# A banded convolution on sixteen 32-by-32 tiles of TensorE instead of four 64-by-64 ones, with the low-rank product moved behind it

## The chip, the cores and the metric

The kernel runs on one core of one Trainium2 chip. The metric is the device time of one execution in microseconds (us), as the median of several. The four runs of the kernel before lie within 0.33% of each other (352.78 to 353.95). Some executions fall in a slower state, in which the granted clock of TensorE (PE) is lower on average. A profiled execution shows a span that is about 1.8 us shorter than the time (352.1 against 353.87 for the kernel before).

## The reference

Two steps on x of 8 batches, 4224 positions and 192 channels:

```python
# 1. causal convolution: 8 heads of 24 channels, 7 softmax weights for each head
out = np.einsum('hk,bskhg->bshg', softmax(weight), x_unf)      # x_unf: 7 shifted copies of x
# 2. low-rank mixing over positions, then two dense layers over channels
h  = xt @ U @ V              # (192 x 4224) @ (4224 x 32) @ (32 x 4224), for each batch
u  = y + h.transpose(0, 2, 1)                                  # y: the convolution's result
ch = np.maximum(u @ w_ch1, 0.0) @ w_ch2                        # 192 -> 768 -> 192
return u + ch
```

## The kernel before

All matrix work is on PE in bf16. 264 tiles of 128 positions are handled in 33 groups of 8 tiles. The main loop has 34 slots. Slot `g` does the first dense layer of group `g` (`w1`), some heads of a later batch's convolution (`conv`), the second dense layer of group `g-1` (`w2`) and the low-rank product of a later group (`h_group`). The kernel holds eight PSUM banks in one pool, and every matmul group takes its bank from it in turn. ACT and DVE empty the banks.

The convolution is a product with a banded matrix: a block of positions times the band, plus a second matmul for the positions that reach over from the block before (`halo`). Before, a block has 64 positions, so a matmul uses a 64-by-64 tile of the array. The four matmuls of one `halo` lie on the four tiles (`tile_position`) and run at the same time: in the trace of before four start within 10 ns (114.091 to 114.101 us), each lasts about 0.35 us, and the next four start from 114.278 us on.

```python
    def conv(b, h, i0, i1, engs):                       # one head
        ...
        pp = [bank(), bank()]
        for halo in range(2):
            for r in range(2):
                for c in range(2):
                    st = 1 - halo + i0 + c
                    nc.tensor.matmul(
                        out=pp[r][HB * c : HB * c + HB, 0 : nn[r] * GS],
                        lhsT=band[HB * r : HB * r + HB, h, HB * halo : HB * halo + HB],
                        rhs=xt[b][HB * r : HB * r + HB, st : st + 2 * nn[r] - 1 : 2, hc],
                        start=(halo == 0), stop=(halo == 1),
                        tile_position=(HB * r, HB * c),
                    )
        ...                                             # ACT or DVE copies pp[r] into y_sb
```

Before the loop stands the prologue: loads, masks, the convolution of batch 0 in two halves, and the transposed u of groups 0 and 1. The rest of the order:

```python
    RELU = ["AA", "AD", "AA", "AD", "AD", "AD"]         # who empties w1's banks: ACT or DVE
    ...
    for k, (i0, i1) in enumerate(XCH):                  # prologue: batch 0 in two halves
        for h in range(H):
            conv(0, h, i0, i1, "AD")
        if k == 0:
            u_layout()                                  # waits for the mask Eq of POOL
            yT[0] = yT_part(0)
        tt_mm(0, ...)
    ...
    for g in range(NG + 1):
        if g + 1 < NG and g > 0:
            h_group(g + 1)                              # low-rank product, one slot ahead
            transp(g + 1)                               # transpose of u by DMA
        if g < NG:
            last = w1(g)
        ...
        for b, ch in loadq.get(g, []):                  # loads of x for a later batch
            ...
        for b, h in convq.get(g, []):
            conv(b, h, 0, NB1, "AA")
        ...
        for k in range(4):
            if g > 0:
                w2(g - 1, k)
            ...
```

## Time and profile before

| before | us |
|---|---|
| median of 3 runs (352.78 to 353.95) | 353.29 |
| profiled span | 352.1 |
| first layer of slot 0 starts | 30.00 |
| slots 0 to 4 | 50.57 |
| slots 5 to 24 | 193.48 |
| slots 25 to 31 (no convolution left but in the first) | 62.21 |
| the rest | 15.85 |

A slot is taken from the start of its first layer to the start of the next slot's. The last five lines add up to the span. All are read from the starts of PE's matmuls in the trace.

These are lines of the profile page of before: the span, PE's busy time and instruction count, the busy share and the granted clock in 40 slices of 8.8 us (tenths, 9 is 90% or more), the queue that brings instructions, and the chain of waits by engine.

```profile
span 352.1 us, 9621 instructions
...
PE 338.9 (96%) x4004; PEld 228.7 (65%) x4004; DVE 246.1 (70%) x500; ACT 191.0 (54%) x409; POOL 56.5 (16%) x98
...
PE   8589899999999999999999999999999999999995
...
PEclk9869899999999999999999999999999999999999
...
q8 instruction: 31, 0.51, 0.6%
...
PE 90%; DVE 4%; DMA 3%; POOL 2%; issue 1%; ACT 0%; POOLq 0%
```

PE is the bound: it is busy in every slice from the sixth on, and 90% of the chain lies on it. Only the first 44 us have something else to give. PE has 4004 matmuls and as many weight loads. The granted clock is below full only in the second, third and fifth slice.

Next is the timeline of PE in one steady slot of before, with two heads of convolution; the columns are start, length, engine, line, operation, and how many instructions were merged.

```profile
114.09 0.88 PE L284 MATMUL ps<-x_sb,band 64*64 64x384 bf16 x16
114.91 4.13 PE L478 MATMUL ps<-W_sb,rl_sb 128*128 128x192 bf16 x48
118.97 0.34 PE L356 MATMUL ps<-tt_sb,V_sb 32*128 32x192 bf16 x8
119.25 4.11 PE L455 MATMUL ps<-uT,W_sb 64*128 64x512 bf16 x36
123.29 0.88 PE L284 MATMUL ps<-x_sb,band 64*64 64x384 bf16 x16
```

From start to start, the convolution of two heads takes 0.82 us (114.09 to 114.91), the second layer 4.06, the product 0.28 and the first layer 4.04: 9.20 in all. There is no wait between them.

Two lines of PE's timeline in the prologue of before:

```profile
17.95 0.42 PE L256 MATMUL ps<-Ur,Eq 32*128 32x288 bf16 x1 [3.75 <-POOL Eq L151]
...
30.00 0.76 PE L455 MATMUL ps<-uT,W_sb 64*128 64x512 bf16 x4
```

PE stood for 3.75 us waiting for a mask that POOL builds, and the first layer started at 30.0 us.

### The profile page before, as it was taken

How to read it: one execution, taken by the hardware profiler on the slowest of the kernel's cores; microseconds unless marked ns; L12 is line 12 of the kernel's file. 1: busy time of each engine (PE TensorE's matmuls, PEld its weight loads, DVE VectorE, ACT ScalarE, POOL GpSimd, SP SyncE). 2: the span in 40 equal slices, each digit the busy share in tenths (PEclk: the TensorE clock that was granted, in tenths of full speed). 3: DMA queues.
4: the chain of work that ended last, by engine and by line, in shares of the span. 5: the costliest groups of instructions: out<-in, count | busy, mean ns of one | idle time of the engine just before them, and what ended most of it. 6: DMA issues, size and time to landing. Idle time of an engine off the chain costs nothing.

```text
span 352.1 us, 9621 instructions
## 1 busy us (share of the span) xinstructions
PE 338.9 (96%) x4004; PEld 228.7 (65%) x4004; DVE 246.1 (70%) x500; ACT 191.0 (54%) x409; POOL 56.5 (16%) x98
## 2 busy tenths in 40 slices
PE   8589899999999999999999999999999999999995
PEld 3354377666667776666577777666767776666675
DVE  6548865677777776666777777676677777777763
ACT  1345465776645554566666554555566644444440
POOL 8592213111101111111111110111000000000000
PEclk9869899999999999999999999999999999999999
DMA  9979989976989899878969897899445454555535
GB/s 110 193 97 158 111 165 147 205 148 152 177 169 165 176 177 181 157 135 153 185 151 180 178 184 150 169 182 177 103 114 131 121 150 118 136 137 134 136 104 166
DMA packets 122922, 53.51 MB, mean 152 GB/s; under 512 B 88160, under 2 KB 122848, under 8 KB 122880
## 3 DMA queue, kind: packets, MB, share of 16 engines
q1 hardware_dynamic: 84656, 38.18, 43.4%
q0 software_dynamic: 38224, 14.73, 37.1%
q8 instruction: 31, 0.51, 0.6%
q14 instruction: 11, 0.09, 0.1%
HBM read 29.49 MB, written 25.95 MB: 157 GB/s over the span
## 4 chain that ended last, share of the span: by engine, by line
PE 90%; DVE 4%; DMA 3%; POOL 2%; issue 1%; ACT 0%; POOLq 0%
PE ps L455 39%; PE ps L478 38%; PE ps L284 6%; DMA x_sb<-in_x_dram 3%; PE ps L356 2%; PE ps L308 2%; DVE u_sb L378 1%; DVE y_sb L299 1%; PE ps L409 1%; POOL Eq L151 1%; DVE rl_sb L467 1%; DVE uT L439 1%; POOL x_sb L76 0%; PE ps L325 0%; DVE out_sb L486 0%
## 5 line engine op out<-in xcount | busy, mean ns | idle before, releaser
L465 ACT ACTIVATE rl_sb<-ps 128x512 bf16<-128x512 f32 x264 | 133.3, 623 | 121.5 <-issue 66.2
L455 PE MATMUL ps<-uT,W_sb 64*128 64x512 bf16 x1188 | 143.6, 380 | 0.8 <-DVE uT L439 0.2
L478 PE MATMUL ps<-W_sb,rl_sb 128*128 128x192 bf16 x1584 | 138.6, 247 | 0.0
L478 PEld LDWEIGHTS <-rl_sb 128*128 128x128 bf16 x1584 | 128.8, 98 | 12.2 <-issue 12.2
L486 DVE TENSOR_TENSOR out_sb<-ps,u_sb 128x384 f32<-128x384 f32 x132 | 73.6, 557 | 77.5 <-PE ps L478 77.5
L455 PEld LDWEIGHTS <-W_sb 64*128 64x128 bf16 x1188 | 64.3, 95 | 69.2 <-issue 14.0
L467 DVE TENSOR_SCALAR rl_sb<-ps 128x512 bf16<-128x512 f32 x132 | 88.1, 689 | 7.1 <-PE ps L455 6.9
L378 DVE TENSOR_TENSOR u_sb<-y_sb,ps 128x192 bf16<-128x192 bf16 (+1 forms) x168 | 66.1, 460 | 0.0
L297 ACT ACTIVATE y_sb<-ps 128x384 bf16<-128x384 f32 (+2 forms) x128 | 52.6, 528 | 0.3
L76 POOL DMA_DIRECT2D x_sb<-in_x_dram x30 | 21.2, 705 | 178.7 <-PE ps L455 163.2
L284 PE MATMUL ps<-x_sb,band 64*64 64x408 bf16 (+3 forms) x576 | 29.5, 335 | 0.0
L284 PEld LDWEIGHTS <-band 64*64 64x64 bf16 x576 | 16.8, 117 | 13.7 <-issue 11.5
L81 POOL DMA_DIRECT2D x_sb<-in_x_dram x30 | 22.1, 736 | 0.0
L356 PE MATMUL ps<-tt_sb,V_sb 32*128 32x192 bf16 x264 | 12.8, 246 | 1.1 <-DVE u_sb L378 0.7
L356 PEld LDWEIGHTS <-V_sb 32*128 32x128 bf16 x264 | 4.8, 92 | 7.2 <-issue 6.8
L318 ACT ACTIVATE tt_hi<-ps 128x192 bf16<-128x192 f32 x9 | 3.0, 330 | 12.0 <-PE ps L308 12.0
L308 PE MATMUL ps<-y_sb,U_sb 128*32 128x192 bf16 x264 | 8.1, 254 | 0.4 <-ACT y_sb L297 0.4
L319 DVE TENSOR_TENSOR tt_lo<-ps,tt_hi 128x192 bf16<-128x192 f32 x9 | 3.2, 357 | 6.1 <-ACT tt_hi L318 6.1
L180 PE MATMUL ps<-zz 128*128 128x512 bf16 x20 | 6.0, 471 | 1.2 <-DVE zz L176 1.2
L308 PEld LDWEIGHTS <-U_sb 128*32 128x32 bf16 x264 | 5.8, 98 | 2.1 <-issue 2.0
L256 PE MATMUL ps<-Ur,Eq 32*128 32x256 bf16 (+1 forms) x16 | 2.2, 410 | 4.6 <-POOL Eq L151 4.6
L299 DVE CAST y_sb<-ps 128x192 bf16<-128x192 f32 (+1 forms) x16 | 5.1, 366 | 1.0 <-PE ps L284 1.0
(48 smaller groups left out, 55.4 us busy)
## 6 DMA issues: line engine op xcount, KB each, us to landing
out_dram<-out_sb SPq DMA_DIRECT2D x132, 192.0 KB, 2.7
x_sb<-in_x_dram POOLq DMA_DIRECT2D x42, 192.0 KB, 4.3
x_sb<-in_x_dram POOLq DMA_DIRECT2D x7, 240.0 KB, 5.5
x_sb<-in_x_dram POOLq DMA_DIRECT2D x7, 216.0 KB, 4.7
W_sb<-in_moe_w_ch_dram POOLq DMA_DIRECT2D x3, 288.0 KB, 6.0
x_sb<-in_x_dram POOLq DMA_DIRECT2D x2, 384.0 KB, 6.3
uT<-u_sb SPq DMA_TRANSPOSE x31, 3.7
x_sb<-in_x_dram POOLq DMA_DIRECT2D x1, 432.0 KB, 9.0
```

What stands on the lines that cost most here:

```text
L76: return nc.gpsimd.dma_start(out=xt[b][0:HB, 1 + i0 : 1 + e0, :], in_=x[b, i0 * HB : e0 * HB, :].rearrange("(j p) d -> p j d", p=HB),)
L81: return nc.gpsimd.dma_start(out=xt[b][HB:P, s0 : i1 + 1, :], in_=x[b, (NB0 - 1 + s0) * HB : (NB0 + i1) * HB, :].rearrange("(j p) d -> p j ...
L284: nc.tensor.matmul(out=pp[r][HB * c : HB * c + HB, 0 : nn[r] * GS], lhsT=band[HB * r : HB * r + HB, h, HB * halo : HB * halo + HB], rhs=xt ...
L297: nc.scalar.activation(out=o, in_=i, func=ACT.Copy)
L308: nc.tensor.matmul(out=p[32 * c : 32 * c + 32, 0:D], lhsT=U_sb[:, j // 4, j % 4, :], rhs=yt[b][:, j, :], start=(n < 4), stop=(n + 4 >= len ...
L356: nc.tensor.matmul(out=banks[pr][:, a * D : (a + 1) * D], lhsT=V_sb[32 * q : 32 * q + 32, (j // 8) * 2 + j % 2, :], rhs=ttb[b][32 * q : 32 ...
L378: nc.vector.tensor_tensor(out=u_group(g)[:, i : i + n, :, hf, :], in0=yt[b][:, run[0] : run[0] + n, :].rearrange("p n (c k) -> p n c k", c=3),
L455: last = nc.tensor.matmul(out=pp[hf][:], lhsT=W1_sb[HB * hf : HB * hf + HB, c, m * P : (m + 1) * P], rhs=uTt[g][HB * hf : HB * hf + HB, :, ...
L465: nc.scalar.activation(out=rl[:, m, hf, :], in_=pp[hf][:], func=ACT.Relu)
L467: nc.vector.tensor_scalar_max(out=rl[:, m, hf, :], in0=pp[hf][:], scalar1=0.0)
L478: nc.tensor.matmul(out=cps[:, a * D : (a + 1) * D], lhsT=rlt[g][:, m, hf, (i + a) * P : (i + a + 1) * P], rhs=W2_sb[:, m, :], start=(m == ...
L486: nc.vector.tensor_tensor(out=o[:].rearrange("p n (c k) -> p n c k", c=3), in0=cps[:, 0 : 2 * D].rearrange("p (n c k) -> p n c k", n=2, c= ...
```

## The change

The intent: make the convolution cheaper on PE by using all sixteen 32-by-32 tiles at once, start the first batch sooner by convolving it quarter by quarter as its loads land, and take waits out of the prologue. In the loop the product moves from ahead of the first layer to between convolution and second layer, two slots ahead. The transposed u of groups 0 and 1 is now summed in PSUM rather than by DVE. The masks are built by DVE. There are two x buffers instead of three. From batch 3 on, a batch's convolution stands one slot sooner than before and its loads two. The core of the diff, with cuts marked:

```diff
-    xs = ctx.enter_context(tc.tile_pool(name="xs", bufs=3))
+    xs = ctx.enter_context(tc.tile_pool(name="xs", bufs=2))
 ...
-    def conv(b, h, i0, i1, engs):
+    def conv(b, hp, rs, engs):                          # a pair of heads, some of the 4 quarters
 ...
-        pp = [bank(), bank()]
-        for halo in range(2):
-            for r in range(2):
-                for c in range(2):
+        pp = {r: bank() for r in rs}
+        for hh in range(2):
+            h = 2 * hp + hh
+            for halo in range(2):
+                for c in range(4):
+                    for r in rs:
+                        st = 1 - halo + c
                         nc.tensor.matmul(
+                            out=pp[r][QB * c : QB * c + QB, ...],
+                            lhsT=band[QB * r : QB * r + QB, h, QB * halo : QB * halo + QB],
+                            rhs=xt[b][QB * r : QB * r + QB, st : st + 4 * nk[r] - 3 : 4, ...],
 ...
+                            tile_position=(QB * r, QB * c),
 ...
-    RELU = ["AA", "AD", "AA", "AD", "AD", "AD"]
+    RELU = ["AD", "AD", "AA", "AD", "AD", "AD"]
 ...
+    for hp in range(4):                                 # prologue: batch 0 in quarters
+        conv(0, hp, [0], "AD"[hp % 2])
+    u_layout()
+    for hp in range(4):
+        conv(0, hp, [1], "AD"[hp % 2])
+    for hp in range(4):
+        conv(0, hp, [2], "AD"[hp % 2])
+    tt_whole(0, tt_mm(0, range(3 * NQ)), "A")
+    for hp in range(4):
+        conv(0, hp, [3], "AD"[hp % 2])
 ...
     for g in range(NG + 1):
-        if g + 1 < NG and g > 0:
-            h_group(g + 1)
-            transp(g + 1)
         if g < NG:
-            last = w1(g)
+            last = w1(g, RELU0 if g < 2 else RELU)
 ...
-            conv(b, h, 0, NB1, "AA")
+            conv(b, hp, [0, 1, 2, 3], "A")
 ...
+        for n in hq.get(g, []):                         # product, two slots ahead
+            h_group(n)
+            transp(n)
 ...
             w2(...)
```

A pair of heads now takes 64 matmuls of 192 or 216 columns where it took 16 of 384 or 408.

## The prediction

> **What bounds it now.** From about 44 us to 348 us TensorE never stops: the busy row shows PE at 95 to 100% in every slice, and the chain of waits is 90% PE (ps L455 39%, L478 38%, conv L284 6%). In the timeline a slot with two conv heads is first layer 4.03 us, conv 0.82, second layer 4.07, low-rank product 0.28: 9.2; a slot without conv takes 8.74, where the first layer waits 0.35 for banks that DVE still empties. Before 44 us the chain is made of loads, POOL's Eq masks (U layout waits for them until 20.0 us), DVE adds (uT, u_sb); the first layer starts at 30.0, its second group at 37.7.
>
> **What the change does.**
> 1. Conv: 64 matmuls of 192 or 216 columns on 16 tiles for two heads, instead of 16 of about 400 columns on 4. In the trace, matmuls on different tiles start 3.4 ns apart, and a round of 192 columns lasts 82 ns: 55 ns of issue against 82 to 93 of streaming. Two heads: 4 rounds plus a mode change, about 0.5 us instead of 0.82. 28 pairs: 9 us of PE time less (estimate). Evictions stay: 16 a batch, ACT, 0.6 us each, one per 0.38 us.
> 2. That gain should mostly turn into waits for PSUM. The product moves between conv and second layer. After the first layer PE now wants 4 banks (conv), 4 or 5 (product), then 1 (second layer), of 8. Reckoned from the slot's start with trace durations: the last relus end at 4.8 us, the conv is done at 4.63 and its first two evictions end at 5.23 and 5.6. The second layer's first bank is (by the built program) one of those: it starts at 5.28 (4-bank product) or 5.66 (5-bank), against 4.85 plus 0.28 for the product elsewhere. Slots 5 to 24: 9.3 to 9.7 us, not better than 9.2. [...] before shows no such PE wait, after should.
> 3. Slots 1 to 4 hold two pairs: eight ACT evictions in a row before the second layer, about 11.3 us instead of 9.9 in slots 3 and 4.
> 4. Slots without conv lose that wait: 8.35 us, 7 times, -2.7 us.
> 5. Prologue: masks on DVE (about 1.5 us) end the wait for Eq; band is 152 wide instead of 280 (14 ops, 0.24 instead of 0.37 us); u of the first groups accumulates in PSUM, no 0.68 us adds; the products of groups 0 and 1 no longer precede the second group. Loads land as before (x near 15 us). First layer starts near 23.5 us.
>
> **Sum.** At the fifth slot about 6 us ahead, slots 5 to 31 about 2 us lost, end 0.3 us gained: **348.0 us**, range 342.5 to 353.5. Faster by over 2%: 0.33; within 2%: 0.65; slower: 0.02.
>
> **What would show it.** Conv group under 0.6 us from its first start to the next group; PE waits at the product and the second layer, released by ACT y_sb and relus; slot time 9.3 to 9.7; first layer near 23.5 us; slots without conv near 8.35.
>
> **What would make it wrong.** Banks released earlier than reckoned (then 340 us); 16 tiles streaming slower than one round per 90 ns; x of batch 1 landing after 33 us, or batch 2's last quarter stuck on POOL's queue behind batch 3's (slower).

The "mode change" of point 1 can be read in before: 0.31 us from the last matmul of the first layer to the first of the convolution (113.784 to 114.091 us) and 0.27 us from the last of the convolution to the second layer (114.642 to 114.908), where the rounds within the convolution start 0.16 to 0.19 us apart and the pairs of first-layer matmuls ahead of it 0.215 us. The 1.5 us for the masks and the 0.24 us for an operation of the band were estimates; after has 1.6 us on DVE (five operations from 9.51 us on) and 0.24 us (ten in 2.36 us from 7.23 us on).

## The result

| | before | after |
|---|---|---|
| median of 4 runs | 353.59 | 367.38 |
| fast runs | 352.78 to 353.95 | 363.88 and 364.80 (slow: 369.97, 370.93) |
| ratio of fast runs | | 1.0307, 95% interval 1.0267 to 1.0347 |
| PE matmuls (and as many weight loads) | 4004 | 5476 |

The change made the kernel 3.1% slower. The two slow runs are left out of the ratio. A ratio is the mean time of one kernel's fast runs over that of the other's of the same rounds, so it is not quite the ratio of the medians. The profiled execution of after was one of the fast ones (363.88 us).

The same stages, from the traces:

| us | predicted | before | after | after minus before |
|---|---|---|---|---|
| first layer of slot 0 starts | near 23.5 | 30.00 | 29.78 | -0.2 |
| slots 0 to 4 | about 51 | 50.57 | 58.05 | +7.5 |
| slots 5 to 24 | | 193.48 | 197.77 | +4.3 |
| slots 25 to 31 | | 62.21 | 60.13 | -2.1 |
| slots 5 to 31 together | 2 lost | 255.69 | 257.90 | +2.2 |
| the rest | 0.3 gained | 15.85 | 16.38 | +0.5 |

The "about 51" is worked out: before is at its slot 5 at 80.57, "about 6 us ahead" is 74.5, less 23.5. So the steady part came out as predicted, in sum. (The parts as the prediction gives them, 6 and 0.3 us gained and 2 lost, make 349.0 us from 353.3, not 348.0; that is small beside the miss.) What was missed is the 88 us before it: after reaches slot 5 at 87.83 us, not 6 us ahead of before but 7.3 behind it.

The page of after, the same lines as above:

```profile
span 362.1 us, 12473 instructions
...
PE 343.7 (95%) x5476; PEld 236.8 (65%) x5476; DVE 260.4 (72%) x521; ACT 182.7 (50%) x371; POOL 35.6 (10%) x60
...
PE   8899899699999999999999999999999999999995
...
PEclk9659999889999999999999999999999999999999
...
q8 instruction: 43, 0.70, 0.8%
```

Three things differ. PE is busier in the first slices, but its clock there is lower (6 and 5 in the second and third). Slice 8 has a hole in the PE row, and the clock is below full there too. And the instruction queue brought 43 packets instead of 31, each of 16384 bytes in both traces; they are called blocks below. The chain of waits of after covers only a quarter of the span, so it is not used here.

Now PE's share of two stretches, by windows, first before, then after. The columns are the stretch, its length, PE's busy time (instructions), the granted clock, the DMA share and GB/s.

```profile
10.00:20.00 10.00, 5.12 (x71) 0.73 1.40 193
20.00:30.00 10.00, 9.05 (x176) 0.76 0.87 99
```

```profile
10.00:20.00 10.00, 9.02 (x244) 0.55 1.34 183
20.00:30.00 10.00, 9.55 (x142) 0.60 1.53 177
```

After removed the wait for the mask: PE is busy for 18.57 of these 20 us instead of 14.17. But its clock is about half. In the trace the clock is 0.5 in one piece from 10.97 to 28.04 us, 17.07 us, which is five times 3.41 us; in before the pieces at 0.5 in the first 45 us last 3.41, 6.83 and 3.41 us (from 11.12, 17.95 and 38.43 us). What that costs stands in the starts of the matmuls: four matmuls of 192 columns on the four tiles of one quarter make a round, and a round takes 82 ns at full clock (from 9.80 us) and 160 ns at half (from 12.49 us). The lines of PE's timeline of after in this stretch:

```profile
9.80 1.69 PE L282 MATMUL ps<-x_sb,band 32*32 32x192 bf16 x64
...
12.49 4.01 PE L282 MATMUL ps<-x_sb,band 32*32 32x192 bf16 x109
17.48 0.98 PE L282 MATMUL ps<-x_sb,band 32*32 32x192 bf16 x19 [0.98 <-issue]
...
19.56 3.06 PE L282 MATMUL ps<-x_sb,band 32*32 32x216 bf16 x64
22.55 1.49 PE L419 MATMUL ps<-ident,y_sb 128*64 128x128 bf16 x24
...
29.78 1.42 PE L454 MATMUL ps<-uT,W_sb 64*128 64x512 bf16 x9
```

The convolution of the last quarter alone takes 3.0 us. The 24 transposes take 1.42 us to the next group, and 0.79 us in a stretch of before where the clock is full (26.80 to 27.59). The first layer starts at 29.78.

"issue" in brackets is a wait for which the profile has no releaser. The largest such wait of after is in slot 3, here with its neighbours:

```profile
63.41 0.26 PE L282 MATMUL ps<-x_sb,band 32*32 32x192 bf16 x3
64.02 1.54 PE L282 MATMUL ps<-x_sb,band 32*32 32x216 bf16 x125 [0.35 <-DMA x_sb<-in_x_dram]
...
67.41 0.90 PE L477 MATMUL ps<-W_sb,rl_sb 128*128 128x192 bf16 x9
70.68 5.86 PE L477 MATMUL ps<-W_sb,rl_sb 128*128 128x192 bf16 x39 [2.38 <-issue]
76.48 4.06 PE L454 MATMUL ps<-uT,W_sb 64*128 64x512 bf16 x36
```

The second layer of this slot takes 9.07 us (67.41 to 76.48) instead of 4.06. 2.62 us is the stall, from one matmul start (68.06) to the next. The rest, about 2.4 us, is the clock, which the trace has at 0.5 from 69.00 to 75.83. There are three more such stalls of over 0.6 us: 1.34 at 16.13, 1.08 at 40.07 and 0.75 at 54.11.

And a steady slot of after, to be set against that of before:

```profile
108.37 4.06 PE L454 MATMUL ps<-uT,W_sb 64*128 64x512 bf16 x36
112.36 0.80 PE L282 MATMUL ps<-x_sb,band 32*32 32x192 bf16 x64
113.09 0.47 PE L367 MATMUL ps<-tt_sb,V_sb 32*128 32x192 bf16 x8
113.71 4.12 PE L477 MATMUL ps<-W_sb,rl_sb 128*128 128x192 bf16 x48
117.77 1.04 PE L454 MATMUL ps<-uT,W_sb 64*128 64x512 bf16 x8
```

The slot takes 9.40 us. The convolution takes 0.73, not the 0.5 predicted. From the start of the product to the second layer it is 0.62 us, of which the product itself took 0.28 in before: 0.34 us is a wait. The second layer starts 5.34 us after the slot; 5.28 was predicted.

### The profile page after: what moved, and what is told of

It is laid out like the page before. It is cut to its first block, busy times and chain, and to the rows that moved or that the text cites. A ratio compares the mean times of both kernels' runs of the same rounds, so it can differ in the third digit from the quotient of the medians.

```text
span 362.1 us, 12473 instructions
## 1 busy us (share of the span) xinstructions
PE 343.7 (95%) x5476; PEld 236.8 (65%) x5476; DVE 260.4 (72%) x521; ACT 182.7 (50%) x371; POOL 35.6 (10%) x60
## 5 line engine op out<-in xcount | busy, mean ns | idle before, releaser
L464 ACT ACTIVATE rl_sb<-ps 128x512 bf16<-128x512 f32 x233 | 124.5, 604 | 128.6 <-issue 73.9
L477 PEld LDWEIGHTS <-rl_sb 128*128 128x128 bf16 x1584 | 132.5, 99 | 11.5 <-issue 6.1
L454 PE MATMUL ps<-uT,W_sb 64*128 64x512 bf16 x1188 | 134.9, 377 | 0.1
L466 DVE TENSOR_SCALAR rl_sb<-ps 128x512 bf16<-128x512 f32 x163 | 107.6, 690 | 26.1 <-PE ps L454 26.1
L454 PEld LDWEIGHTS <-W_sb 64*128 64x128 bf16 x1188 | 56.2, 94 | 67.8 <-issue 6.0
L485 DVE TENSOR_TENSOR out_sb<-ps,u_sb 128x384 f32<-128x384 f32 (+1 forms) x133 | 71.0, 551 | 35.9 <-PE ps L477 35.1
L245 ACT ACTIVATE y_sb<-ps 128x384 bf16<-128x384 f32 (+1 forms) x120 | 50.7, 511 | 8.1 <-PE ps L282 6.0
L80 POOL DMA_DIRECT2D x_sb<-in_x_dram x32 | 26.0, 815 | 128.8 <-PE ps L454 113.9
L282 PEld LDWEIGHTS <-band 32*32 32x32 bf16 x2048 | 24.4, 92 | 16.2 <-issue 13.4
L282 PE MATMUL ps<-x_sb,band 32*32 32x192 bf16 (+1 forms) x2048 | 32.6, 261 | 2.2 <-issue 1.8
L367 PE MATMUL ps<-tt_sb,V_sb 32*128 32x192 bf16 x264 | 19.4, 246 | 4.4 <-ACT y_sb L245 3.4
L74 POOL MEMSET x_sb<- 32x96 uint32 x7 | 1.2, 172 | 61.7 <-PE ps L367 27.2
```

The source lines that it names most:

```text
L80: return nc.gpsimd.dma_start(out=xt[b][QB * q : QB * q + QB, s0:s1, :], in_=x[b, blk * QB : (blk + s1 - s0) * QB, :].rearrange("(j p) d -> ...
L245: nc.scalar.activation(out=out, in_=in_, func=ACT.Copy)
L282: nc.tensor.matmul(out=pp[r][QB * c : QB * c + QB, 0 : nk[r] * 2 * GS].rearrange("p (k a) -> p k a", a=2 * GS)[:, :, hh * GS : hh * GS + G ...
L367: nc.tensor.matmul(out=banks[pr][:, a * D : (a + 1) * D], lhsT=V_sb[32 * q : 32 * q + 32, (j // 8) * 2 + j % 2, :], rhs=ttb[b][32 * q : 32 ...
L454: last = nc.tensor.matmul(out=pp[hf][:], lhsT=W1_sb[HB * hf : HB * hf + HB, c, m * P : (m + 1) * P], rhs=uTt[g][HB * hf : HB * hf + HB, :, ...
L464: nc.scalar.activation(out=rl[:, m, hf, :], in_=pp[hf][:], func=ACT.Relu)
```

## The experiments

Three theories were to be told apart. A: the granted clock goes by how much of the array works, so the quarter-by-quarter convolution, which uses 4 of 16 tiles at a time, lets the clock fall although PE is busy. B: PE runs out of instructions, because the new convolution takes so many, and waits for their blocks. C: x comes late, because two buffers instead of three bunch the loads. Medians of before on the chips used were 353.28 to 354.06 us. A median below is over all runs of a kernel, and where a median holds slow runs, that is said. The stages of all runs, from their traces:

| us | first layer starts | slots 0-4 | slots 5-24 | slots 25-31 | rest | span |
|---|---|---|---|---|---|---|
| before | 30.00 | 50.57 | 193.48 | 62.21 | 15.85 | 352.1 |
| after | 29.78 | 58.05 | 197.77 | 60.13 | 16.38 | 362.1 |
| e1_hot_full | 30.06 | 55.75 | 197.76 | 60.13 | 15.99 | 359.7 |
| e2_hot_small | 34.81 | 55.78 | 197.74 | 60.12 | 15.95 | 364.4 |
| e3_xs3 | 28.80 | 54.57 | 197.75 | 60.12 | 16.57 | 357.8 |
| e4_late | 30.22 | 59.07 | 193.96 | 61.92 | 16.63 | 361.8 |
| e5_halves (slow) | 28.87 | 64.69 | 197.77 | 60.13 | 17.05 | 368.5 |
| e6_conv64 | 23.93 | 53.29 | 194.29 | 60.13 | 15.97 | 347.6 |
| e7_conv32_only | 32.50 | 52.48 | 191.71 | 62.14 | 15.86 | 354.7 |
| e8_split | 29.63 | 62.42 | 209.52 | 60.13 | 17.00 | 378.7 |
| e9_conv64_xs3 | 24.18 | 51.72 | 194.29 | 60.13 | 15.99 | 346.3 |
| e10_conv64_xs3_early | 23.63 | 50.85 | 193.13 | 61.08 | 16.01 | 344.7 |
| e11_loads_moved | 28.38 | 64.19 | 197.76 | 60.13 | 16.54 | 367.0 |
| e12_shift | 30.30 | 57.49 | 197.73 | 60.12 | 16.27 | 361.9 |

All gave correct results.

### e1_hot_full and e2_hot_small: dummy matmuls in the prologue's convolution

The changed kernel, with one matmul of zeros per bank ahead of each convolution group of batch 0. The real group overwrites what it wrote. e1 uses the whole array, e2 one 32-by-32 tile of the row group that the real matmuls use.

```diff
+        if b == 0:
+            for r in rs:
+                nc.tensor.matmul(out=pp[r][:], lhsT=zz[:, 0:P], rhs=zz[:], start=True, stop=True)
# e2: out=pp[r][0:QB, :], lhsT=zz[QB*r : QB*r+QB, 0:QB], rhs=zz[QB*r : QB*r+QB, :],
#     tile_position=(QB*r, 0)
```

> The changed kernel with one matmul of zeros on the whole array (128x128, 512 columns) before each of the 16 conv groups of the first batch, into the bank that the group then overwrites. Theory A (the clock was halved from 11 to 28 us because a conv of one quarter uses only 4 of the 16 tiles, all in one row group[...]): granted clock over 14 to 28 us at least 0.85 instead of 0.5, the conv of the second and third quarter takes under 4.5 us instead of 5.9 in spite of the extra matmuls, the first layer starts at 26 us or sooner instead of 29.8, time 2 to 5 us below the changed kernel's 364. Rival B (the engine waits for loads and evictions there, the low clock is only a sign of idling and costs nothing): first layer starts at the same 29.8 us or up to 3.5 us later, time 364 to 368.

> As e1_hot_full, but the 16 extra matmuls of zeros are 32x32 on the same row group as the conv that follows, 512 columns each: TensorE is as busy in time, the array as empty. Theory A (occupied array counts): the clock stays at 0.5 from 11 us on, the extra work runs at half speed (0.43 us each, up to 6.9 us in all), the first layer starts 2 to 7 us later than 29.8, time 366 to 371. Theory A2 (busy time counts, idling between evictions brought the clock down): the clock recovers as in e1_hot_full and the time falls like that one's.

The half speed that e2 expects (0.43 us for 512 columns) agrees with the 160 ns for 192 columns of after, which make 0.427.

Measured: e1 365.1 us (ratio 1.0289, interval 1.0221 to 1.0356), e2 367.69 (1.0406, 1.0368 to 1.0444). PE by windows, first e1, then e2:

```profile
10.00:20.00 10.00, 10.00 (x210) 1.00 1.38 192
20.00:30.00 10.00, 9.33 (x194) 1.00 1.57 183
```

```profile
10.00:20.00 10.00, 10.00 (x197) 0.58 1.37 189
20.00:30.00 10.00, 10.00 (x157) 0.50 1.61 186
```

With as many dummies, and PE busy all the time from 10 to 20 us in both (from 20 to 30 us e1 is even the less busy, 9.33 against 10.00), the clock stays full with full-array dummies and is half with small ones. In e2 the first layer starts 4.8 us later than in e1 (34.81 against 30.06). So it is not PE's busy time that holds the clock up, and the half clock costs time. Theory A stands, with one caution: a full-array dummy differs from a small one in rows and columns both, and the two were not separated. The gain that e1 was expected to show did not come, neither in the start of the first layer (30.06 us, where at most 26 was expected) nor clearly in the time: its fast runs are 361.53, 363.66 and 366.53 us against 363.88 and 364.80 of after (a fourth, 375.64, was slow). Both numbers lie near those of rival B; what speaks against B is the pair e1 and e2, not e1 alone. Each dummy took 0.32 us with the change of tiling, so 16 of them about 5.1 us, and its convolution started 1.2 us later. So the dummies ate what the clock gave.

### e3_xs3: three x buffers again

```diff
-    xs = ctx.enter_context(tc.tile_pool(name="xs", bufs=2))
+    xs = ctx.enter_context(tc.tile_pool(name="xs", bufs=3))
```

> The changed kernel with three buffers of x instead of two. Theory C (batch 3's first load waits on POOL's queue for batch 1's buffer, five quarters then go out back to back at 54 to 57 us, the DMA is full, TensorE's instruction blocks and the last quarter of batch 2 come late): no burst at 54 us; the stalls of TensorE of 0.75 us at 54 and 2.6 us at 68 us, the wait for x of 0.6 us at 63 and the half clock after 69 us are gone; the fifth slot starts at 81 to 83.5 us instead of 87.8; time 357 to 361. The stalls at 16 us (1.35) and 40 us (1.08) stay. Rival D (the stalls come from the number of instructions alone, whatever the loads): stalls of the same size remain, time 363 to 365.

Measured: fast runs of 359.62 and 361.10 us, ratio 1.0188 (1.015 to 1.0227); two more, 365.52 and 365.66, were slow, and the median of all four is 363.31. Slot 5 starts at 83.37 us in the profile, which is a fast run. Batch 3's loads no longer wait for batch 1's buffer, and no longer leave together with batch 2's last quarter. The wait for x in slot 3 is gone, and so is the large stall at 68 us. The stalls at 16 (1.12 us), 39 (1.94) and 55 us (0.75) stay. So theory C is real, but it is the smaller part: the clock and the other stalls remain. One of them in the timeline of e3:

```profile
38.26 1.09 PE L282 MATMUL ps<-x_sb,band 32*32 32x192 bf16 x66
41.03 0.30 PE L282 MATMUL ps<-x_sb,band 32*32 32x192 bf16 x12 [1.68 <-issue]
```

A group of convolution is cut in two in its midst, and nothing that the profile knows of held it. (The window begins inside the group, so its first matmuls are not counted in x66.)

### e4_late: the product behind the second layer

```diff
         for b, hp in convq.get(g, []):
             conv(b, hp, [0, 1, 2, 3], "A")
-        for n in hq.get(g, []):
-            h_group(n)
-            transp(n)
         ...                                             # the loop of w2
+        for n in hq.get(g, []):
+            h_group(n)
+            transp(n)
```

> The changed kernel with the low-rank product put behind the second layer in each slot (still two slots ahead), so that conv is followed by the second layer at once, as before the change. Theory E (in the steady slots TensorE waits at the product and at the second layer for banks that the last relus and the conv evictions hold): slots 5 to 24 fall from 9.4 to 9.6 us to 9.05 to 9.2; slots 3 and 4 lose their wait at the product (1.4 us each); slots without conv rise by up to 0.4; time 354 to 359. Rival F (the conv's own pace, 8.3 ns a matmul, sets the slot): slots stay at 9.4 or more, time 362 to 366.

Measured: 363.56 us, ratio 1.0262 (1.0222 to 1.0302). Slots 5 to 24 fell by 3.8 us to 193.96. The wait ahead of the second layer is gone, but the first layer behind the product rose from 3.99 to between 4.33 and 4.40 us, probably because DVE's adds still hold the product's banks: in before, where the product also stands ahead of the first layer, weight loads of the first layer wait 16 times, 7.9 us in all, for the adds into `u_sb`. So slots of 9.77 us became 9.4 to 9.5, those of 9.39 only 9.34, and slots 25 to 31 gave 1.8 us back. Little of it showed in the time, since the first five slots grew to 59.07, with a stall of 4.0 us in slot 3. The wait for banks was in part removed and in part only moved, and this did not take the loss away.

### e5_halves: batch 0 in halves

```diff
-        conv(0, hp, [0], "AD"[hp % 2])
+        conv(0, hp, [0, 1], "AD")                       # then u_layout, the first product,
-        conv(0, hp, [1], "AD"[hp % 2])                  # and conv(0, hp, [2, 3], "AD")
...
```

> The changed kernel with the first batch in two halves (two quarters, 8 of 16 tiles, at a time) instead of quarter by quarter; the order in the prologue is that of before (U layout, transposes of group 0 and the first product of U after the first half). Theory A (low array occupancy halves the clock): the conv of the batch needs half as many rounds, 4 to 5 us of TensorE time at half clock go away, and with half the array in use the clock may recover earlier than 28 us; the first layer starts at 25 to 27.5 us, time 358 to 361. Rival B (loads and evictions set the pace): the first layer starts at 29 us or later, time as the changed kernel, 363 to 365.

Measured: 365.4 us (fast runs 364.36 to 365.98, one slow), ratio 1.0315 (1.0272 to 1.0359). The clock was still 0.5 at 12.8 to 16.2 and 19.7 to 33.3 us, and the first layer started at 28.87, between what the two theories expected. Eight of sixteen tiles did not hold the clock up here; but PE was busy for only 8.41 of the 10 us from 20 to 30, so part of this may be idling. The profile of this run fell in the slow state, so its length of stages isn't compared further. One thing it shows: its slots 5 to 31 take 257.90 us as in after, so this slow run lost nothing there: it was not slowed by a lower clock throughout.

### e6_conv64: the 64-by-64 convolution, all else of the change kept

The changed kernel with `conv`, the layout of x and the two halves of batch 0 taken from before; masks, u in PSUM, the place of the product, two x buffers and `RELU` as in after.

```diff
-            conv(b, hp, [0, 1, 2, 3], "A")
+            conv(b, 2 * hp, 0, NB1, "AA")
+            conv(b, 2 * hp + 1, 0, NB1, "AA")
...                                                      # conv and the loads of x as in before
```

> The changed kernel with the old conv on four 64x64 tiles and the old x layout by halves, all else of the change kept (masks on DVE, u of the first groups in PSUM, product two slots ahead behind the conv, relus' split, two x buffers). If the loss comes from the 32x32 conv (clock in the prologue, instruction blocks): clock not at 0.5 throughout 11 to 28 us, first layer at 24 to 26.5 us, none of the stalls of 0.7 us and more without a semaphore, instruction blocks 31 instead of 43, slots 5 to 24 at 9.3 to 9.6; time 351 to 357. If the loss comes from the rest of the change: time 361 to 365.

Measured: 349.75 us, ratio 0.9877 (0.9844 to 0.991). PE by windows of e6:

```profile
10.00:20.00 10.00, 9.31 (x205) 0.83 1.42 197
20.00:30.00 10.00, 9.48 (x113) 1.00 1.51 176
```

And its timeline:

```profile
11.39 2.85 PE L288 MATMUL ps<-x_sb,band 64*64 64x192 bf16 x64
...
23.93 4.42 PE L456 MATMUL ps<-uT,W_sb 64*128 64x512 bf16 x36
```

The clock dips for one 3.41 us piece only, and the first layer starts at 23.93 us. This is the run that weighs the new convolution, with its layout of x and its quarters, against the rest. Between the profiles of e6 and after lie 14.5 us: 5.85 before the first layer, 4.76 in slots 0 to 4, 3.48 in slots 5 to 24, and 0.4 at the end. Taking the new convolution out of the change takes the whole loss out; what else was changed gains 1.2%. But its cost depends on what stands around it: 14.5 us here, 11.5 with three x buffers (e3 against e9), and 2.6 in the kernel before (e7 below), by the spans. So it is a loss together with the rest, not a fixed price. There is no stall of over 0.6 us without a semaphore in e6, and its instruction queue brought 31 packets, as in before.

### e7_conv32_only: before with nothing but the new convolution

The kernel before with `conv` on 32-by-32 tiles and x by quarters, batch 0 in halves; everything else, the product ahead of the first layer too, as before.

> The kernel before with the 32x32 conv and x by quarters alone (first batch in two halves of two quarters; masks on POOL, product before the first layer, three x buffers as before). If the 32x32 conv is what costs: stalls without a semaphore of 0.7 to 2.5 us appear near the first three conv groups, each ending 1.2 to 1.5 us after a 16 KB instruction block; conv 0.73 us instead of 0.82 in the steady slots, which stay at 9.1 to 9.2; first layer not earlier than 30 us; time 354 to 360. If the conv is a gain by itself and the rest of the change costs: time 345 to 350.

Measured: 356.19 us, ratio 1.0055 (1.002 to 1.0089). The short steady slots are 9.11 us instead of 9.20, so slots 5 to 24 gain 1.8 us. That is the pair's 0.73 instead of 0.82 us and nothing more. The first layer starts 2.5 us later, with the clock at 0.5 from 13.5 to 23.7 and from 27.2 to 37.4 us. PE still waits for the mask there (6.02 us, up to 18.61), so part of the first stretch is idling too. One stall without a semaphore came, of 1.07 us at 59.96, where several were expected. Only the prologue and the first slots make it slower, by 0.5% in all.

### e8_split: twice the matmuls, the same columns

From batch 3 on, each matmul of the convolution is cut in two along its columns (96 and 96, or 96 and 120).

```diff
+            cuts = {r: [0, 4, nk[r]] if b > 2 else [0, nk[r]] for r in rs}
+            for piece in range(2 if b > 2 else 1):
...                                                      # columns k0 to k1 of each piece
```

> The changed kernel with every conv matmul of batches 3 to 7 cut in two (96 and 96 or 120 columns instead of 192 or 216): twice the matmuls and weight loads, the same columns. If the conv's pace is set by the number of instructions (8.3 ns a pair after the first 32): conv groups in slots 5 to 24 stream for 1.0 to 1.1 us instead of 0.54, slots 9.7 to 10.1, time 6 to 12 us above the changed kernel's 364 to 365, and 10 more instruction blocks; new stalls if such a block comes late. If columns or PSUM writes set it: conv groups stay near 0.54 us and the time near 365.

Measured: 380.85 us, ratio 1.0754 (1.0685 to 1.0822), beyond what was expected. A group in the timeline of e8:

```profile
127.86 1.25 PE L285 MATMUL ps<-x_sb,band 32*32 32x96 bf16 x128
129.05 0.34 PE L372 MATMUL ps<-tt_sb,V_sb 32*128 32x192 bf16 x8
```

From start to start the group takes 1.19 us instead of 0.73, for the same columns. So the group is bound by the number of its instructions and not by the columns that stream (each matmul has its weight load, and the two were not told apart). Within a group of 64 (in after, from 112.362 us) the trace has the first 32 matmuls mostly 3 to 4 ns apart and, after a pause of 124 ns, the others 8.3 ns apart; with 128 in e8 the remaining 96 go on at 8.3 ns. Stalls without a semaphore now come in the steady part too (0.83 us at 118.54, 0.63 at 265.51, 0.76 at 277.51), and the instruction queue brought 53 packets.

### e9_conv64_xs3 and e10_conv64_xs3_early: to a better version

e9 is e6 with three x buffers. e10 is e9 with the product ahead of the first layer and the `RELU` of before.

```diff
-    xs = ctx.enter_context(tc.tile_pool(name="xs", bufs=2))            # e9
+    xs = ctx.enter_context(tc.tile_pool(name="xs", bufs=3))
-    RELU = ["AD", "AD", "AA", "AD", "AD", "AD"]                        # e10
+    RELU = ["AA", "AD", "AA", "AD", "AD", "AD"]
+        for n in hq.get(g, []):                                        # now ahead of w1(g)
+            h_group(n)
+            transp(n)
```

> e6_conv64 with three x buffers. In e6 TensorE waited 1.0 us for x of batch 2 (queued behind batch 3's blocked load) and 1.5 us for a transpose in the burst of loads that followed. Theory C (two buffers make the burst): both waits go, slot 5 starts 2 to 3 us earlier than in e6 (88 us), time 346 to 348. If the waits have another cause, time stays at 349 to 350.

> e9 with the low-rank product ahead of the first layer again, as before the change (still two slots ahead), and the relu split of before in the steady slots. If the place of the product behind the conv costs 0.3 to 0.5 us a slot (waits for banks) and saves 0.35 in slots without conv: slots 5 to 24 at 9.2 instead of 9.4 to 9.6, slots 3 and 4 at 9.9 instead of 11.2, slots without conv at 8.7; time 340 to 344, which would beat both kernels. If the place does not matter: time as e9.

Measured: e9 348.04 us, ratio 0.9839 (0.9794 to 0.9884); e10 347.25, ratio 0.9802 (0.9777 to 0.9827). e6 had waited 1.0 us for x and 1.5 us for a transpose in slot 3; e9 has neither, and its first five slots are 1.6 us shorter. e10 has the lowest time of all versions, 2.0% under before, which leaves the verdict at 2% unclear. It was expected at 340 to 344 and is only 0.8 us under e9, 0.2%, which is within what runs of one kernel differ by. The expectation took 9.2 us for all of slots 5 to 24, but only the plain ones take that: before itself has a mean of 9.67. Against e9, slots 5 to 24 fell by 1.16 us and slots 25 to 31 rose by 0.95, so the place of the product, with the `RELU` of before, matters little. A steady slot of e9, with the product where the change put it:

```profile
96.21 4.06 PE L456 MATMUL ps<-uT,W_sb 64*128 64x512 bf16 x36
100.20 0.88 PE L288 MATMUL ps<-x_sb,band 64*64 64x384 bf16 x16
101.01 0.39 PE L369 MATMUL ps<-tt_sb,V_sb 32*128 32x192 bf16 x8
101.35 4.12 PE L479 MATMUL ps<-W_sb,rl_sb 128*128 128x192 bf16 x48
105.40 1.90 PE L456 MATMUL ps<-uT,W_sb 64*128 64x512 bf16 x16
```

This slot takes 9.19 us against 9.40 in after, though its convolution takes 0.81 instead of 0.73. It makes up for it behind the convolution: from product to second layer 0.34 us instead of 0.62. The old convolution finishes its banks two by two, one head after the other, so ACT starts to empty the first pair while the second is being filled (4.58 us into the slot, with the convolution on PE until 4.80). The new one finishes all four banks of a pair of heads only at the end (ACT starts at 4.80, PE leaves the convolution at 4.72).

### e11_loads_moved: the loads of x elsewhere

e3 with batch 2's loads all in slot 2 and batch 3's in slots 3, 3, 4 and 4, so that no load of x runs from 33 to 50 us.

```diff
-                loadq.setdefault(max(0, slots[0] - 5 + q), []).append((b, q))
+                at = {2: 2, 3: 3 + q // 2}.get(b, max(0, slots[0] - 5 + q))
+                loadq.setdefault(at, []).append((b, q))
```

> The changed kernel with three x buffers (e3_xs3), and batch 2's four loads issued in slot 2 instead of slots 0 and 1, batch 3's in slots 3 and 4: no load is in flight from 33 to 50 us. If the stalls are instruction blocks queued behind loads: the stall of 1.1 to 2.3 us that the changed kernel, e3, e4 and e8 all show at 39 to 41 us is gone or under 0.3 us, and one of 1 to 4 us appears instead where the moved loads run (53 to 70 us). If TensorE's instructions come too slowly whatever the DMA carries: the stall at 40 us stays.

Measured: one run, 368.8 us, state unknown. The stall near 39 us is gone: the packet of the block that is needed there started at 35.46 us, with no load of x under way, instead of at 38.81 as in after, and PE did not wait. A stall of 2.57 us stands at 73.81 instead, among the moved loads, and x itself came late (waits of 2.06 and 4.12 us between 62.9 and 69.0 us). So in this run the stall went where the loads went, and moving them is no cure.

### e12_shift: other block boundaries

In the traces of all runs so far, the matmuls and weight loads that PE had started when a stall of over 0.6 us without a semaphore began were counted: 446, 702, 1214, 1726, 2238, 4030, 10430 and 10942. That is 446 plus a multiple of 256 each time, in 22 stalls of seven kernels; one of the 22, in e7, came 2 instructions sooner. This run is e3 with 16 small matmuls of zeros in the warm-up, which move every later instruction by 32 places.

```diff
     for _ in range(20):
         nc.tensor.matmul(out=wps[:], lhsT=zz[:, 0:P], rhs=zz[:], start=True, stop=True)
+    for _ in range(16):
+        nc.tensor.matmul(out=wps[:, 0:64], lhsT=zz[:, 0:P], rhs=zz[:, 0:64], start=True, stop=True)
```

> The changed kernel with three x buffers, plus 16 small zero matmuls (64 columns) in the warm-up. They move every later TensorE instruction 32 places (16 matmuls and 16 weight loads) further from the start, and so the boundaries of the 16 KB blocks to other instructions. In all traces so far every stall without a semaphore of over 0.6 us came when 446 plus a multiple of 256 matmuls and weight loads had started (or 2 less). Theory (TensorE waits for the next block of instructions; the boundary fell where a whole conv group follows): the stalls near 39 (1.94 us) and 55 us (0.75 us) are gone, as in the two runs with 16 zero matmuls in the conv; if one stays, it is again at 446 plus a multiple of 256. First five slots 51.5 to 52.7 us instead of 54.57, slots 5 to 31 unchanged at 257.9, total 359 to 362. Rival (the stalls come from what the memory traffic of the loads does at those moments, wherever the boundaries are): stalls of the same sum at the same conv groups, first five slots 54 to 55 us, total 362 to 364.

Measured: 363.45 us, ratio 1.0282 (1.0247 to 1.0317). Its stalls came at 446 and at 1726 started instructions, so at the same places in the count though at other matmuls of the program. So the place of a stall goes with the count and not with the matmul (packets of 16384 bytes, one for 256 instructions, are 64 bytes for each). But the gain didn't come: the stall near 39 us is gone, the one in slot 2 grew to 3.89 us, from 52.88 to 56.77 us, and the clock was 0.5 from 55.12 to 61.95. PE's timeline of e12:

```profile
51.49 1.65 PE L284 MATMUL ps<-x_sb,band 32*32 32x192 bf16 x128
56.77 4.02 PE L479 MATMUL ps<-W_sb,rl_sb 128*128 128x192 bf16 x24 [3.63 <-issue]
60.72 1.49 PE L312 MATMUL ps<-y_sb,U_sb 128*32 128x192 bf16 x33
```

The packet of the block was under way from 54.21 to 55.25 us, after 4 us in which stores and transposes alone had kept the DMA engines over 100% by the trace's reckoning (shares of 1.11 and 1.22 from 50 to 52 and 52 to 54 us). So the place of a stall is set by the count, and its length by when the block's packet gets through. The expectation had only the first half.

The traces show why blocks came late in after and not in before. In before each packet starts about one block ahead, when PE has just begun the block before the one that it brings (from 54 instructions short of that point to 86 past it). A block there lasts at least 8.4 us, which is time enough. Ahead of the four stalls of after a block lasted only 2.8 to 5.2 us, and the packet started 0.9 to 4.2 us after that point. In e8, at 118.54 us, the packet started in time, but the block lasted only 1.5 us: there the pace alone made the stall. Three further waits stand at 2238 started instructions (2.32 us in e1, 1.45 in e2, 0.92 in e12). The profile puts them down to ACT, but each ended 1.4 to 1.5 us after a block's packet, as the others do, so they are probably stalls of the same kind.

## Why the prediction was wrong

Point by point, in its own words:

- **Point 5, "First layer starts near 23.5 us": failed, by 6.3 us.** All the work that it takes out of the prologue went out: the wait for the mask is gone, and PE is busy for 18.57 us of 20. The step that failed is the cost of the prologue's work on PE: the prediction has no term for the clock (its one figure for a round of 192 columns, 82 ns, is that of full clock), and the change put the work at half clock for 17.07 us (160 ns for a round). One quarter of the convolution works on 4 of 16 tiles. e6, with the whole array in use, starts at 23.93, and e1 and e2 show that the clock goes with how much of the array works, not with PE's busy time: from 20 to 30 us PE was busy for 9.33 of 10 us at a clock of 1.00 in e1 and for 10.00 at 0.50 in e2. In after it was busy for 9.55 there, at 0.60.
- **"At the fifth slot about 6 us ahead": failed, by 13.3 us.** 6.3 of these are point 5. The other 7.1 are in slots 0 to 4 (58.05 instead of 51). There the trace has stalls of 1.08, 0.75 and 2.62 us, 2.4 us of half clock after the last of them, and a wait of 0.60 us for x. The stalls were not in the prediction at all: it let PE go on as fast as its work and its semaphores allowed, and had no term for fetching the instructions. The traces count them: with 256 to a block (the step between the stalls, under e12), 5476 matmuls and 5476 weight loads are 42.8 blocks, and 43 packets came; 8008 in before are 31.3, and 31 came. They cost no such stall in before, e6, e9 and e10, but they did in after: 128 matmuls of convolution with their loads are a whole block, and PE took 1.58 us for such a group in slot 4 (80.47 to 82.05), while the packet of a block alone takes 0.9 to 1.8 us, and the next matmul started 1.4 to 1.5 us after it had ended (1.39, 1.39, 1.51 and 1.46 us in the four stalls of after).
- **"batch 2's last quarter stuck on POOL's queue behind batch 3's": named as a risk, came true.** Batch 3's quarters waited for batch 1's buffer and went out in a burst with it. With the third buffer (e3) the first five slots are 3.5 us shorter, in part because the block of slot 3 then gets through in time.
- **Point 1, "about 0.5 us instead of 0.82": wrong in size, 0.73 measured.** The 3.4 ns between matmuls were right for the first 32 only; the others start 8.3 ns apart. The 28 pairs save 0.09 us each, 2.5 us in all and not 9. Why the pace changes after 32 was not shown.
- **Point 2, the wait for PSUM banks: right.** 9.39 to 9.78 us in plain steady slots (9.3 to 9.7 predicted), second layer at 5.34 (5.28). That the second number is so close is in part luck: the convolution ended 0.1 us later than reckoned, and ACT's eviction took 0.49 us instead of 0.6. The runs show where it counts: e7 gains 0.09 us a slot from the new convolution where no bank is waited for (9.11 against 9.20 in before), and after loses 0.2 against e9 where one is (9.40 against 9.19). Slots 5 to 31 lost 2.2 us, as predicted, although the gain of point 1 was smaller: the waits would have taken the rest of it too (argued from the sum, not run).
- **Point 3, "about 11.3 us" in slots 3 and 4: right where no stall fell in.** Slot 4 took 11.35; slot 3 took 17.40 in after and 11.69 in e3, which has neither the stall nor the wait for x.
- **Point 4, slots without convolution: right, a little smaller.** Mostly 8.53 us instead of 8.73; 8.35 was predicted, and 2.1 us were gained and not 2.7.

What stays open: whether rows or columns of the array count for the clock, and how many are enough (eight tiles were not, in e5); what passes between the end of a block's packet and the next matmul (1.39 to 1.52 us in the stalls of after and in that of e12 in slot 2); how much of a packet's delay is the loads (e11 is a single run); and what sets apart the slow runs of after (369.97 and 370.93), of which there is no profile.

## What to carry to other kernels

A cost measured at full clock holds only where the change keeps the clock up: here small tiles that left most of the array empty went with half of it while PE looked busy (0.50 with PE busy for 10.00 of 10 us in e2), so read the granted clock beside the busy row before believing a saving. Splitting work into more and smaller matmuls had a price here in instructions (10952 matmuls and weight loads instead of 8008), in issue (8.3 ns for a matmul with its load after the first 32) and in 16 KB blocks (43 instead of 31) that were fetched while the DMA also carried the data. Of this change, the prologue's part was worth keeping (masks on DVE, the first u summed in PSUM; together, not tested one by one, the first layer starts 6.1 us sooner in e6 than in before), with 64-by-64 tiles and three x buffers: 348.04 us with the product in its new place, 347.25 in its old (a difference within the noise), against 353.75.
